# A unit of attention inserted in two places instead of three, its last two steps in the gate's or the value's memory bank

## The chip, the cores and the metric

One NeuronCore of a Trainium2 chip runs the whole program. The time is in device microseconds (us), from three executions of each kernel; their median is what the prediction is about. TensorE (PE) multiplies matrices into PSUM, a memory of eight banks of 128 x 512 numbers; VectorE (DVE) and ScalarE (ACT) read results from there; SyncE (SP) issues the transfers.

## What is computed

Local attention with a few global tokens, followed by two feed-forward layers:

```python
# 4 batches, 8 heads, 512 local and 32 global tokens, 64 per head
out_g = softmax(q_g k_all^T / 8) v_all
out_l = softmax([q_l k_g^T, q_l k_l^T masked to |i - j| <= 32] / 8) [v_g, v_l]
x = rows of out_g, out_l              # 2176 x 512 (heads side by side)
x = (silu(x w_gate) * (x w_val)) w_out        # inner width 1536
out = prelu(x w_in, alpha) w_out2             # inner width 2048
```

All numbers are float32; the weights are split into a high and a low part, and each product of the feed-forward layers is made of three passes (high x high, high x low, low x high).

## The kernel before, in words

The program has three stages. In the first (up to about 405 us of the profiled execution) attention and the first feed-forward layer run interleaved; in the second and third, a blocked product with fewer multiplications finishes the first layer and does the second layer. The change lies in the first stage alone.

`visit1` goes over the twelve blocks `f` of the inner width for one batch of 512 tokens: a gate product (12 matmuls of 128 x 512 into bank `g`), its SiLU on ACT into `sg`, a value product (12 matmuls into bank `v`), the product of both on DVE (`t`), a split of it into high (ACT) and low (DVE) part `h`, and a product with the output weights (`down`, 12 matmuls into the banks `acc0` to `acc3`). Three batches are done in this way, 36 blocks in all. Ahead of each of the three products `pump()` is called. It may insert a step of attention, and it always moves the preparation of the weights on: a load, a conversion of 64-bit numbers on ACT and DVE, a split, a store.

Attention of batches 1 to 3, and the global tokens of all batches, is a list of 20 units: 12 `Local` (a pair of heads) and 8 `Global`. A unit has four parts on PE: `s` (scores into the banks `a0` and `a1`; then a masked maximum on DVE and an exponential on ACT), `t` (eight or six transposes of the exponentials, copied by ACT to `pt`), `pv` (the product with the values; DVE scales it into `o`), and `to` (a transpose of `o`, copied out by ACT). `apump` runs one step of a pipeline over units: step 0 the scores of unit k, step 1 the transposes of unit k-1, step 2 `to` of unit k-3 and `pv` of unit k-2. `pumper` says how many steps are due by each call. Every part takes its bank from `att_bank`, which alternates between `a0` and `a1`. Attention of batch 0 stands ahead of all this (the head) and is spread over all banks.

None of this is issued at once. `Planner` records every instruction of the first stage and then lists them by engine, from the data dependencies, a due time and a cost for each; an instruction that must not be split from its neighbours is in one `atom`. So what the code says is an order of wishes, and the order on an engine is the planner's; it stands below in the part on the change. Nearly every instruction of this stage bears line L273 in the profile, the line at which the planner issues; the tiles' names tell them apart. The names: `g<-xa,w` gate product, `v<-xa,w` value product, `acc<-h,w` down product, `a<-qk` scores, `a<-ident,e` transposes of exponentials, `a<-v,pt` value product of attention, `a<-ident,o` the last transpose.

Of the kernel before, what the change touches and what calls it, by code (L numbers as in the profile page):

```python
# [31 lines left out]
GWIN = (1, 4, 13, 15, 7, 10)  # L32
NG = len(GWIN)
P = dict(
    SLACK=60.0, LOOK=0.1, SWITCH=4.0, MARGIN=0.5, HEAT=8, TINY=90, ND=3, NR=3, LAG=6,
    wr0=0.75, wr2=0.5, wr3=0.75, wr4=0.6, wr5=0.2,
    ns1=33, ns2=34, ns3=32, g1=1.0, g2=1.1, g3=1.0,
    lo0=0.0, lo1=0.0, lo2=0.0, lo3=0.0, hi0=0.0, hi1=0.25, hi2=0.25, hi3=0.5,
    wl0=2, wl1=2, wd=2, tsim=False,
    hq0=0.0, hq1=0.0, hq2=0.0, hq3=0.0, pr_s=0, pr_pv=0, pr_conv=0, pr_hilo=0, pr_st=0, pr_ld=0, pr_h=0,  # L40
# [282 lines left out]
def kernel(  # L323
# [13 lines left out]
    HEAT, ND, NR, LAG = (P[i] for i in ("HEAT", "ND", "NR", "LAG"))  # L337
# [51 lines left out]

    att_tags = {"list": ["a0", "a1", "acc0", "acc1", "acc2", "acc3", "g", "v"], "i": 0}  # L390

    def att_bank():
        t = att_tags["list"][att_tags["i"] % len(att_tags["list"])]
        att_tags["i"] += 1
        return bank(t)
# [49 lines left out]
    class Local(Unit):  # L445
# [59 lines left out]
                nc.vector.reciprocal(out=rc[:, :, 0], in_=rc[:, :, 0])  # L505

        def pv(self):
            o = att_bank()
            with nc.atom():
                for t in range(4):  # L510
                    for h in range(2):
                        for c in range(4):
                            nc.tensor.matmul(
                                out=o[32 * c:32 * c + 32, 128 * t + D * h:128 * t + D * h + D],
                                lhsT=self.pt[:, h, 128 * t + 32 * c:128 * t + 32 * c + 32],
                                rhs=self.pair.v[:, h, 4 * t + c],
                                start=True,
                                stop=True,
                            )
            rc = self.rc  # L520
            self.o = attp.tile([128, 8, D], F32, tag="o", name="o", bufs=1)
            nc.vector.tensor_tensor(
                out=self.o, in0=o.rearrange("p (a d) -> p a d", d=D), in1=rc.to_broadcast([128, 8, D]), op=ALU.mult
            )

        def to(self):
            b, p = self.pair.b, self.pair.p
            t = att_bank()
            rows = self.o.rearrange("p a d -> p (a d)")
            with nc.atom():  # L530
                for i in range(0, 512, 128):
                    nc.tensor.transpose(t[:, i:i + 128], rows[:, i:i + 128], ident)
            if b == 0:
                hi, lo = (xa[:, i, p, 0:S] for i in range(2))
                nc.scalar.activation(out=hi, in_=t, func=ACTF.Copy)
                nc.vector.tensor_tensor(out=lo, in0=t, in1=hi, op=ALU.subtract)
            elif b < B - 1:
                nc.scalar.activation(
                    out=yp[b][:, :, p], in_=t.rearrange("p (a c) -> p a c", a=2), func=ACTF.Copy
                )  # L540
            else:
                for hf in range(2):
                    nc.scalar.activation(out=yh(b, hf)[:, p], in_=t[:, 256 * hf:256 * hf + 256], func=ACTF.Copy)

    class Global(Unit):
# [58 lines left out]
                nc.vector.reciprocal(out=rc, in_=rc)  # L604

        def pv(self):
            o = att_bank()
            with nc.atom():
                for i, w in enumerate(GWIN):
                    for j in range(4):  # L610
                        nc.tensor.matmul(
                            out=o[32 * j:32 * j + 32, 0:D],
                            lhsT=self.pt[:, 128 * i + 32 * j:128 * i + 32 * j + 32],
                            rhs=self.pairs[j // 2].v[:, j % 2, w],
                            start=(i == 0),
                            stop=(i == NG - 1),
                        )
            rc = self.rc
            self.o = attp.tile([128, 8, D], F32, tag="o", name="og", bufs=1)
            for h in range(2):  # L620
                nc.vector.tensor_scalar(
                    out=self.o[:, h], in0=o[:, 0:D], scalar1=rc, scalar2=None, op0=ALU.mult
                )

        def to(self):
            t = att_bank()
            nc.tensor.transpose(t[:, 0:128], self.o.rearrange("p a d -> p (a d)")[:, 0:128], ident)
            ks, cols = slice(2 * self.grp, 2 * self.grp + 2), slice(32 * self.b, 32 * self.b + 32)
            for h in range(2):
                rows = slice(D * h, D * h + D)  # L630
                src = t[rows, 0:128].rearrange("p (k h q) -> p k h q", k=2, h=2)[:, :, h]
                nc.scalar.activation(out=yg[rows, ks, cols], in_=src, func=ACTF.Copy)
# [4 lines left out]
    for b in range(B):  # L637
        for g in range(2):
            if b:
                units += [Local(pairs[b][p]) for p in (2 * g, 2 * g + 1)]  # L640
            units.append(Global(b, g))
        mark.append(3 * len(units))

    st = {"k": 0, "head": True, "w2": 0.0, "w2i": 0}
    due = {}
    rest = {f: deque(pairs[b][p] for b in range(1, B) for p in range(4)) for f in ("load_qk", "load_v")}

# [10 lines left out]
                    getattr(rest[f].popleft(), f)()  # L658

    def apump(mid=None):  # L660
        k, m = divmod(st["k"], 3)
        u, v, w, x = (units[i] if 0 <= i < len(units) else None for i in (k, k - 1, k - 2, k - 3))
        if m == 0 and u:
            u.s()
            later(1, lambda: reload_pairs(u, "load_qk"))
        if m == 1 and v:
            v.t(0)
            v.t(1)
        if m == 2 and x:
            x.to()  # L670
        if m == 2 and w:
            w.pv()
            later(1, lambda: reload_pairs(w, "load_v"))
        for f in due.pop(st["k"], []):
            f()
        if mid:
            mid()
        st["k"] += 1
# [8 lines left out]

    def dbl_tile():
        i = ring["d"] = (ring["d"] + 1) % ND
        if i == 2 and st["k"] < mark[2] - 4:  # L690
            return yp[2].rearrange("p h m c -> p (h m c)").bitcast(I64)
        return dblp.tile([128, 1024], I64, tag="dbl", name="dbl")

# [13 lines left out]
    def wload(now=False):  # L707
        if wq and not wq[0][3]:
            keys, src, pool, _, age = wq[0]
            if st["w"] < age + P["wage"] and not now:  # L710
                return False
            wq.popleft()
            at = pool.next("w")
            t = wtile(pool)
            if callable(src):
                src(t, at)
                return True
            with pr("ld"):
                nc.sync.dma_start(out=t.bitcast(F32), in_=src)
            put(keys, t)  # L720
            return True
        if wq and len(wloaded) < (ND if st["k"] < mark[2] - 4 else 2):
            keys, src, pool, _, _ = wq.popleft()
            raw = dbl_tile()
            with pr("ld"):
                nc.sync.dma_start(out=raw.rearrange("p (i c) -> p i c", i=2), in_=src)
            wloaded.append([keys, raw, pool, st["w"]])
            return True
        return False
# [189 lines left out]
    def visit1(b, fs, last, pump, after_f=None, boundary=None):  # L919
# [13 lines left out]
                after_f(f, "o")  # L933

        for i, f in enumerate(fs):
            pump()
            g = bank("g")
            mm12(g, weight((1, f, "g")), 0, S)
            sg = work.tile([128, 512], F32, tag="sg", name="sg")
            with pr("h"):  # L940
                nc.scalar.activation(out=sg, in_=g, func=ACTF.Silu)
            pump()
            v = bank("v")
            mm12(v, weight((1, f, "v")), 0, S)
            if after_f:
                after_f(f, "gv")
            t = work.tile([128, 512], F32, tag="t", name="t")
            h = hs[f] = hp.tile([128, 2, 512], F32R, tag="h", name="h")
            nc.vector.tensor_tensor(out=t, in0=v, in1=sg, op=ALU.mult)
            nc.scalar.activation(out=h[:, 0], in_=t, func=ACTF.Copy)  # L950
            soon.append(lambda h=h, t=t: nc.vector.tensor_tensor(out=h[:, 1], in0=t, in1=h[:, 0], op=ALU.subtract))
            pump()
            if i:
                down(fs[i - 1])
        if boundary:
# [85 lines left out]
    if True:  # L1041
# [44 lines left out]
        def pumper(nslots, target, wrate=1.0, g=1.0):  # L1086
# [1 line left out]
            c = [0]  # L1088
            st["wr"] = 0.0

            def pump():
                c[0] += 1
                goal = k0 + (target - k0) * (min(c[0], nslots) / nslots) ** g
                mid = wpump
# [44 lines left out]
        p = pumper(P["ns2"], mark[3] + LAG, P["wr2"], P["g2"])  # L1139
        visit1(1, GB, False, p, after_f=summing(reload(GA, GB)))  # L1140
        visit1(1, GA, True, p, after_f=summing(lambda f, ps: None), boundary=lambda: xprep(2))
        p = pumper(P["ns3"], mark[4] + 9, P["wr3"], P["g3"])
        visit1(2, GA, False, p, after_f=reload(GB, GA))

        ops1, w3, place, sums = {}, {}, {}, {}
# [23 lines left out]
        def before_third(f, ps):  # L1169
# [12 lines left out]

            wq.append((None, take, wgv, False, st["w"]))
            if f == GB[4]:
                assert st["k"] >= mark[4] + 9
                tags = iter(("e", "e", "pt", "pt"))
                sums.update(x_sums(2, lambda: attp.tile([128, 1024], F32, tag=next(tags))[:, 0:2 * N3]))

# [14 lines left out]
        visit1(2, GB, True, p, after_f=before_third, boundary=third)  # L1203
        while wq:
            wload(True)
        assert st["k"] >= mark[4] + 9 and not stores
        nc.flush()
        attp_pool.release()
        attc.release()
# [376 lines left out]
```

## Time and profile before

| | before |
|---|---|
| median of three runs | 885.64 us (882.5 to 888.14) |
| profiled execution | 882.67 us, span 880.9 us, mean granted clock 0.993 |
| PE busy | 865.6 us (98%) |
| DVE busy | 690.1 us (78%) |
| ACT busy | 527.1 us (60%) |
| DMA of q1 | 238.19 MB, 71.6% of 16 engines |

The span is the time from the first to the last instruction of one profiled execution; the execution's own time lies 1.8 us above it, and 3.0 us below the median of the runs. PE is busy nearly all the time by the profile's count, in which a matmul that waits behind another is busy too; whether PE is at its peak is read from the distance between the starts of matmuls.

### The profile page before, as it was taken

What the parts mean: (1) busy time and instruction counts of PE and PEld (TensorE: products, weight loads), DVE (VectorE), ACT (ScalarE), POOL (GpSimd) and SP (SyncE); (2) the same over time, 40 slices, a digit from 0 to 9 for tenths busy, and PEclk for the clock granted to TensorE, in tenths of its full rate; (3) what the DMA queues carried; (4) which work ended last, traced back from release to release, by engine and by line L of the source; (5) the groups of instructions that cost most, each with busy time, mean ns of one, the idle gap of its engine ahead of it and who ended that gap; (6) DMA issues with size and microseconds to landing.
All of it is one profiled execution on the core that took longest, in us unless ns stands there. A gap on an engine that the chain in (4) does not pass through costs nothing.

```text
span 880.9 us, 17473 instructions
## 1 busy us (share of the span) xinstructions
PE 865.6 (98%) x6946; PEld 750.5 (85%) x6946; DVE 690.1 (78%) x1441; ACT 527.1 (60%) x1051; POOL 0.7 (0%) x6
## 2 busy tenths in 40 slices
PE   7899999999999999999999999999999999999997
PEld 6677778888788777888999999988999988999996
DVE  4897999989877857597766697777896777967776
ACT  6899999878586877654333346343645434553442
POOL 0000000000000000000000000000000000000000
PEclk8999999999999999999999999999999999999999
DMA  9899899899969799985566576364474645585631
GB/s 350 327 399 405 346 363 379 321 366 384 414 240 353 282 334 337 371 296 183 169 246 227 186 273 239 144 244 186 193 279 178 257 168 214 218 301 214 273 144 61
DMA packets 41666, 239.31 MB, mean 272 GB/s; under 512 B 4848, under 2 KB 5488, under 8 KB 19312
## 3 DMA queue, kind: packets, MB, share of 16 engines
q1 hardware_dynamic: 41584, 238.19, 71.6%
q8 instruction: 55, 0.90, 0.4%
q14 instruction: 27, 0.22, 0.1%
HBM read 183.38 MB, written 54.79 MB: 270 GB/s over the span
## 4 chain that ended last, share of the span: by engine, by line
PE 89%; DMA 5%; ACT 2%; DVE 2%; issue 1%; SPq 0%; ACTq 0%; DVEq 0%
PE ps_acc L1456 21%; PE acc L273 11%; PE g L273 10%; PE ps_g L1245 9%; PE ps_v L1245 9%; PE v L273 9%; PE ps_a L1245 8%; PE a L273 6%; PE ps_acc L1302 3%; PE ps_a L1302 2%; DMA dbl<-in_w_dram 1%; DMA qk<-in_qk_dram 1%; DMA w2so<-dbl 1%; DMA w2sx<-dbl 1%; DMA yp<-in_w_dram 1%
## 5 line engine op out<-in xcount | busy, mean ns | idle before, releaser
L1456 PE MATMUL ps_acc<-w,hring 128*128 128x512 f32 x816 | 194.2, 391 | 0.0
L1456 PEld LDWEIGHTS ps_acc<-w,hring 128*128 128x128 f32 x816 | 152.0, 188 | 30.1 <-ACT hring L1425 0.3
L273 PE MATMUL g<-xa,w 128*128 128x512 f32 x432 | 107.7, 397 | 1.0 <-ACT sg L273 0.4
L273 PE MATMUL v<-xa,w 128*128 128x512 f32 x432 | 107.0, 396 | 0.0
L273 PE MATMUL acc<-h,w 128*128 128x512 f32 x432 | 106.1, 394 | 0.0
L1420 ACT ACTIVATE r<-c 128x384 f32<-128x384 f32 (+1 forms) x96 | 47.9, 498 | 93.2 <-DVE c L1253 93.2
L1461 DVE TENSOR_TENSOR oacc<-ps_acc,oacc 128x512 f32<-128x512 f32 x119 | 81.9, 691 | 21.9 <-PE ps_acc L1456 20.7
L273 PEld LDWEIGHTS g<-xa,w 128*128 128x128 f32 x432 | 79.0, 188 | 20.8 <-ACT sg L273 1.5
L273 PEld LDWEIGHTS acc<-h,w 128*128 128x128 f32 x432 | 79.8, 188 | 18.6 <-issue 1.8
L273 PEld LDWEIGHTS v<-xa,w 128*128 128x128 f32 x432 | 79.3, 188 | 18.4 <-issue 1.4
L1425 ACT ACTIVATE hring<-g 128x384 fp32r<-128x384 f32 (+1 forms) x96 | 48.6, 506 | 55.8 <-DVE g L1422 55.5
L1426 DVE TENSOR_TENSOR hring<-g,hring 128x384 fp32r<-128x384 f32 (+1 forms) x96 | 51.1, 532 | 18.9 <-ACT hring L1425 16.1
L1422 DVE SCALAR_TENSOR_TENSOR g<-g,nal,r 128x384 f32<-128x384 f32 (+1 forms) x96 | 56.8, 591 | 10.6 <-ACT g L1421 10.0
L273 ACT ACTIVATE e<-e,mx 128x128 f32<-128x128 f32 (+1 forms) x136 | 57.2, 423 | 10.6 <-DVE mx L273 10.3
L273 ACT ACT_TABLE_LOAD x46 | 59.0, 1283 | 5.6 <-PE g L273 4.1
L1421 ACT ACTIVATE g<-c 128x384 f32<-128x384 f32 (+1 forms) x96 | 47.9, 499 | 13.7 <-DVE hring L1426 13.7
L1245 PE MATMUL ps_g<-xa,w 128*128 128x320 f32 (+1 forms) x288 | 53.4, 319 | 0.2
L1245 PE MATMUL ps_v<-xa,w 128*128 128x320 f32 (+1 forms) x288 | 53.2, 319 | 0.1
L1245 PE MATMUL ps_a<-w 128*128 128x384 f32 (+1 forms) x288 | 51.4, 326 | 0.0
L1245 PEld LDWEIGHTS ps_g<-xa,w 128*128 128x128 f32 x288 | 47.1, 188 | 1.9 <-ACT p L1261 0.4
L1245 PEld LDWEIGHTS ps_v<-xa,w 128*128 128x128 f32 x288 | 46.9, 188 | 1.6 <-DVE u L1269 0.4
L1245 PEld LDWEIGHTS ps_a<-w 128*128 128x128 f32 x288 | 47.9, 188 | 0.1
(209 smaller groups left out, 1403.1 us busy)
## 6 DMA issues: line engine op xcount, KB each, us to landing
dbl<-in_w_dram SPq DMA_DIRECT2D x28, 1024.0 KB, 7.7
w<-w2so SPq DMA_DIRECT2D x24, 1024.0 KB, 5.3
w<-w2sx SPq DMA_DIRECT2D x24, 1024.0 KB, 4.8
w<-w2ss SPq DMA_DIRECT2D x24, 1024.0 KB, 6.8
v<-in_v_dram SPq DMA_DIRECT2D x15, 1024.0 KB, 10.8
qk<-in_qk_dram SPq DMA_DIRECT2D x14, 688.0 KB, 8.7
w2sx<-dbl SPq DMA_DIRECT2D x8, 1024.0 KB, 5.9
w2so<-dbl SPq DMA_DIRECT2D x8, 1024.0 KB, 9.2
```

The lines of the kernel that those rows point to most:

```text
L273: last[o.eng] = getattr(getattr(self.nc, o.eng), o.op)(*o.args, **o.kw)
L1245: nc.tensor.matmul(out=o[:, 0:n], lhsT=left(name, a, k), rhs=x[name][:, b, k, 0:n], start=(i == 0), stop=(i == 5),)
L1302: mm = nc.tensor.matmul(out=o, lhsT=a, rhs=x, start=(first and e == 0 and not second), stop=((j, f, e) == (NF1 // 2 - 1, 0, 2) and i not i ...
L1420: nc.scalar.activation(out=rr, in_=u, func=ACTF.Relu)
L1421: nc.scalar.activation(out=g, in_=u, func=ACTF.Relu, scale=-1.0)
L1422: nc.vector.scalar_tensor_tensor(out=g, in0=g, scalar=nal[:, i:i + 1], in1=rr, op0=ALU.mult, op1=ALU.add)
L1425: nc.scalar.activation(out=hi, in_=g, func=ACTF.Copy)
L1426: nc.vector.tensor_tensor(out=lo, in0=g, in1=hi, op=ALU.subtract)
L1456: nc.tensor.matmul(out=o, lhsT=a, rhs=x, start=(i == 0), stop=(i == 5))
L1461: nc.vector.tensor_tensor(out=oacc[tb], in0=o, in1=oacc[tb], op=ALU.add)
```

## The change

`apump` has two steps instead of three: in step 0 stand `pv` of unit k-2 and the scores of unit k, in step 1 the transposes of unit k-1 and `to` of unit k-2. `pv` and `to` no longer take `a0` or `a1`: they take the bank that `pump` names, `v` ahead of the gate product, `g` ahead of the value product and ahead of `down`. The counts of steps that other rules use (`mark`, `LAG`, the limits for the third buffer of raw weights and for the last sums) are fitted to two steps per unit, and the steps are spread over 35 and 34 calls instead of 34 and 32 in the second and third batch.

```diff
--- before.py
+++ after.py
@@ -32,9 +32,9 @@
-    SLACK=60.0, LOOK=0.1, SWITCH=4.0, MARGIN=0.5, HEAT=8, TINY=90, ND=3, NR=3, LAG=6,
+    SLACK=60.0, LOOK=0.1, SWITCH=4.0, MARGIN=0.5, HEAT=8, TINY=90, ND=3, NR=3, LAG=2,
     wr0=0.75, wr2=0.5, wr3=0.75, wr4=0.6, wr5=0.2,
-    ns1=33, ns2=34, ns3=32, g1=1.0, g2=1.1, g3=1.0,
+    ns1=33, ns2=35, ns3=34, g1=1.0, g2=1.1, g3=1.0,
...
+    def side_bank():
+
+        return bank(st["side"]) if st["side"] else att_bank()
+
     def att_bank():
...
         def pv(self):
-            o = att_bank()
+            o = side_bank()
...
         def to(self):
             b, p = self.pair.b, self.pair.p
-            t = att_bank()
+            t = side_bank()
...
-        mark.append(3 * len(units))
-
-    st = {"k": 0, "head": True, "w2": 0.0, "w2i": 0}
+        mark.append(2 * len(units))
+
+    st = {"k": 0, "side": None, "head": True, "w2": 0.0, "w2i": 0}
...
     def apump(mid=None):
-        k, m = divmod(st["k"], 3)
-        u, v, w, x = (units[i] if 0 <= i < len(units) else None for i in (k, k - 1, k - 2, k - 3))
+        k, m = divmod(st["k"], 2)
+        u, v, w = (units[i] if 0 <= i < len(units) else None for i in (k, k - 1, k - 2))
+        if m == 0 and w:
+            w.pv()
+            later(1, lambda: reload_pairs(w, "load_v"))
         if m == 0 and u:
             u.s()
             later(1, lambda: reload_pairs(u, "load_qk"))
         if m == 1 and v:
             v.t(0)
             v.t(1)
-        if m == 2 and x:
-            x.to()
-        if m == 2 and w:
-            w.pv()
-            later(1, lambda: reload_pairs(w, "load_v"))
+        if m == 1 and w:
+            w.to()
...
-        if i == 2 and st["k"] < mark[2] - 4:
+        if i == 2 and st["k"] < mark[2] - 3:
...
         for i, f in enumerate(fs):
-            pump()
+            pump("v")
             g = bank("g")
...
-            pump()
+            pump("g")
             v = bank("v")
...
-            pump()
+            pump("g")
             if i:
                 down(fs[i - 1])
...
-            def pump():
+            def pump(side):
+                st["side"] = side
                 c[0] += 1
...
-        p = pumper(P["ns3"], mark[4] + 9, P["wr3"], P["g3"])
+        p = pumper(P["ns3"], mark[4] + 4, P["wr3"], P["g3"])
```

The planner makes another order of it. On PE, from the first gate product of the first stage to its last `down` product, attention stood in 63 places between large products, with 18 joints of two parts in one place; now it stands in 52 places with 30 joints. On ACT the table loads fall from 46 to 42. Each instruction of the work itself is there as before, on each engine, with the bank alone changed.

First place, ACT at the start of the first stage, from the high part of the second weight tile on (`sg` is the SiLU, `e` the exponential of a global unit, `pt` the copy of transposes, `raw`, `dbl`, `y`, `yp` conversions of weights, `w` and `h` high parts). Before:

```order
L273 ACTIVATE e_115,sm_117<-e_115,mx_119 128x768
L273 ACT_TABLE_LOAD
L273 ACTIVATE sg_148<-g_103 128x512
L273 ACTIVATE dbl_111<-dbl_111 128x1024
L273 ACTIVATE h_151<-t_150 128x512
L273 ACTIVATE w_135<-raw_132 128x2x512
L273 ACTIVATE y_139<-yp_95 128x1024
L273 ACTIVATE yp_95<-yp_95 128x1024
L273 ACTIVATE pt_123<-a_113 128x512
L273 ACTIVATE pt_123<-a_114 128x256
L273 ACTIVATE sg_148<-g_103 128x512
```

Now:

```order
L273 ACT_TABLE_LOAD
L273 ACTIVATE sg_148<-g_103 128x512
L273 ACTIVATE dbl_111<-dbl_111 128x1024
L273 ACTIVATE h_151<-t_150 128x512
L273 ACT_TABLE_LOAD
L273 ACTIVATE e_115,sm_117<-e_115,mx_119 128x768
L273 ACTIVATE w_135<-raw_132 128x2x512
L273 ACTIVATE y_139<-yp_95 128x1024
L273 ACTIVATE yp_95<-yp_95 128x1024
L273 ACT_TABLE_LOAD
L273 ACTIVATE sg_148<-g_103 128x512
L273 ACTIVATE pt_123<-a_113 128x512
```

The first SiLU now stands ahead of the exponential of 768 columns, two more table loads stand ahead of the second SiLU, and the two copies to `pt` stand behind it. On PE at this place the scores of a local unit stood between the second value product and the third gate product; now the transposes of the first global unit alone stand there.

Second place, PE in the second batch. Before, a `down` product, transposes, a gate product, then the last transpose of a global unit and the value product of a local one, in `a0` and `a1` (a_113, a_114):

```order
L273 MATMUL acc_121<-h_151,w_143 128x512 x3
L273 MATMUL acc_122<-h_151,w_143 128x512 x3
L273 MATMUL acc_125<-h_151,w_143 128x512 x3
L273 MATMUL acc_126<-h_151,w_143 128x512 x3
L273 MATMUL a_114<-ident,e_115 128x128 x4
L273 MATMUL a_113<-ident,e_115 128x128 x4
L273 MATMUL g_103<-xa,w_135 128x512 x12
L273 MATMUL a_114<-ident,o_130 128x128
L273 MATMUL a_113<-v_110,pt_124 32x64 x32
```

Now:

```order
L273 MATMUL g_103<-xa,w_135 128x512 x12
L273 MATMUL acc_121<-h_152,w_143 128x512 x3
L273 MATMUL acc_122<-h_152,w_143 128x512 x3
L273 MATMUL acc_125<-h_152,w_143 128x512 x3
L273 MATMUL acc_126<-h_152,w_143 128x512 x3
L273 MATMUL g_103<-v_110,pt_124 32x64 x32
L273 MATMUL a_113<-ident,e_115 128x128 x4
L273 MATMUL a_114<-ident,e_115 128x128 x4
L273 MATMUL v_129<-ident,o_130 128x128 x4
L273 MATMUL g_103<-xa,w_136 128x512 x12
L273 MATMUL v_129<-xa,w_136 128x512 x12
```

The value product of attention stands in the gate's bank (g_103), joined to the transposes, and the last transpose stands in the value's bank (v_129); one `down` product lies between the gate product and the former, and one gate product between the latter and the value product that takes its bank again.

## Rows read from the trace of the kernel before

**Rows 1.** Waits of TensorE (PE): total us, how many times, longest us.

```profile
PE g L273 <- ACT sg L273: 0.4, 2, 0.2
```

**Rows 2.** Busy us of each engine in one stretch, granted clock, DMA share, GB/s.

```profile
60.00:80.00 20.00, 20.00 (x220) 15.51 (x220) 16.87 (x43) 19.86 (x43) 0.00 (x0) 1.00 1.00 392
```

**Rows 3.** PE in order of time: start us, length us, what, from 157 us.

```profile
157.45 2.88 PE L273 MATMUL v<-xa,w 128*128 128x512 f32 x12
160.17 2.88 PE L273 MATMUL acc<-h,w 128*128 128x512 f32 x12
162.98 1.54 PE L273 MATMUL a<-qk 64*32 64x256 f32 x32
164.45 3.01 PE L273 MATMUL acc<-h,w 128*128 128x512 f32 x12
167.30 2.88 PE L273 MATMUL g<-xa,w 128*128 128x512 f32 x12
...
173.53 3.00 PE L273 MATMUL g<-xa,w 128*128 128x512 f32 x12
176.37 0.27 PE L273 MATMUL a<-ident,o 128*128 128x128 f32 x1
176.57 1.10 PE L273 MATMUL a<-v,pt 128*32 128x64 f32 x64
```

**Rows 4.** PE in order of time, from 294 us.

```profile
294.81 0.27 PE L273 MATMUL a<-ident,o 128*128 128x128 f32 x1
294.84 3.00 PE L273 MATMUL g<-xa,w 128*128 128x512 f32 x12
```

**Rows 5.** PE in order of time, from 41 to 53 us; idle time before in brackets.

```profile
41.81 3.04 PE L273 MATMUL g<-xa,w 128*128 128x512 f32 x12 [0.20 <-ACT sg L273]
44.69 0.82 PE L273 MATMUL a<-ident,e 128*128 128x128 f32 x6
45.26 2.99 PE L273 MATMUL v<-xa,w 128*128 128x512 f32 x12
48.97 1.16 PE L273 MATMUL a<-qk 64*32 64x128 f32 x64 [0.72 <-ACT pt L273]
50.05 3.02 PE L273 MATMUL g<-xa,w 128*128 128x512 f32 x12
```

**Rows 6.** ScalarE (ACT) in order of time, from 39 to 49 us.

```profile
39.87 1.28 ACT L273 ACT_TABLE_LOAD   x1
41.16 0.60 ACT L273 ACTIVATE sg<-g 128x512 f32<-128x512 f32 x1
...
44.39 1.06 ACT L273 ACTIVATE w<-raw 128x1024 fp32r<-128x1024 f32 x1 [0.84 <-DVE raw L273]
45.97 1.15 ACT L273 ACTIVATE y<-yp 128x1024 f32<-128x1024 f32 x1 [0.52 <-DMA yp<-in_w_dram]
...
48.07 0.85 ACT L273 ACTIVATE pt<-a 128x512 f32<-128x512 f32 x2
48.81 0.60 ACT L273 ACTIVATE sg<-g 128x512 f32<-128x512 f32 x1
```

**Rows 7.** PE in order of time: one gate product, one value product of attention.

```profile
132.83 3.02 PE L273 MATMUL g<-xa,w 128*128 128x512 f32 x12
...
370.73 0.88 PE L273 MATMUL a<-v,pt 128*32 128x64 f32 x48
```

**Rows 8.** ACT in order of time: the SiLU of two gate products.

```profile
142.77 0.60 ACT L273 ACTIVATE sg<-g 128x512 f32<-128x512 f32 x1
...
171.56 0.60 ACT L273 ACTIVATE sg<-g 128x512 f32<-128x512 f32 x1
```

**Rows 9.** VectorE (DVE) in order of time: the scaling of one value product.

```profile
375.34 0.47 DVE L273 TENSOR_SCALAR o<-a,rc 128x64 f32<-128x64 f32 x2
```

**Rows 10.** TensorE's busy us (instructions), granted clock, DMA share, GB/s in two stretches.

```profile
24.00:28.00 4.00, 2.36 (x86) 1.00 1.00 407
28.00:32.00 4.00, 3.06 (x66) 0.57 0.68 217
```

More of the change, by code (lines that the diff above doesn't have):

```diff
@@ L606, in pv @@
         def pv(self):
-            o = att_bank()
+            o = side_bank()
             with nc.atom():
@@ L625, in to @@
         def to(self):
-            t = att_bank()
+            t = side_bank()
             nc.tensor.transpose(t[:, 0:128], self.o.rearrange("p a d -> p (a d)")[:, 0:128], ident)
@@ L721, in wload @@
             return True
-        if wq and len(wloaded) < (ND if st["k"] < mark[2] - 4 else 2):
+        if wq and len(wloaded) < (ND if st["k"] < mark[2] - 3 else 2):
             keys, src, pool, _, _ = wq.popleft()
@@ L1184, in before_third @@
             if f == GB[4]:
-                assert st["k"] >= mark[4] + 9
+                assert st["k"] >= mark[4] + 4
                 tags = iter(("e", "e", "pt", "pt"))
@@ L1205 @@
             wload(True)
-        assert st["k"] >= mark[4] + 9 and not stores
+        assert st["k"] >= mark[4] + 4 and not stores
         nc.flush()
```

## The prediction

> **What bounds the kernel now.** I read the waits of TensorE first. Its idle time is small and lies nearly all in the first 50 us; a SiLU, for one, makes it wait 0.4 us in the whole program [rows 1]. Then the busy times by stretch: from 60 to 80 us TensorE is busy 20.00 of 20 us, at a granted clock of 1.00, while ACT is busy 19.86 us and the DMA engines all the time [rows 2]. Since a waiting matmul can count as busy, I went to the starts in order of time. Two products of twelve matmuls that follow each other start 2.72 us apart (157.45 to 160.17) [rows 3], and nowhere in the stretch from 50 to 400 us that I went through is a distance longer by more than the small joints counted below and some 0.3 us at single places. So TensorE is the bound of the first stage, and it has no slack: this change can win only by fewer joints or by the few waits at the start, and it can lose wherever TensorE must wait for a bank.
>
> **Joints (likely nothing).** Where attention interrupts large products, the steady distance of 2.72 us grows. Ahead of scores it is 2.81 us (160.17 to 162.98), and the product behind them needs 2.85 us (164.45 to 167.30): 0.09 + 0.13 = 0.22 us for such a place. A place with transposes costs 0.12 us (173.53 to 176.37 is 2.84) [rows 3]. The new order has 11 places fewer (52 for 63): 11 x 0.12 to 0.22 = 1.3 to 2.4 us saved. But it has 12 joints of small parts more (30 for 18). One last transpose followed by a value product takes 0.20 us to the next start (176.37 to 176.57) [rows 3]; the same transpose followed by a large product takes 0.03 us (294.81 to 294.84) [rows 4]. So such a joint costs 0.17 us, and 12 of them 2.0 us. The net is between 0.4 us saved and 0.7 us lost; other kinds of joints I have no row for, and bound each by 0 and 0.25 us, which gives 2.4 us saved to 1.7 us lost. I take 0.
>
> **The start of the stage (1.5 us lost).** Before, between the second gate product (41.81) and the third (50.05) stand transposes, a value product and the scores of a local unit, which waited 0.72 us for a copy on ACT and took 1.08 us [rows 5]. In the new order the scores come behind the third gate product, so TensorE has only the value product and the transposes: from 41.81 the gate product takes 2.88 us, the value product about 2.72, the transposes 0.57, and it is ready at about 48.0. It needs the second SiLU, which empties the bank. Before, that ended at 48.81 + 0.60 = 49.41. Now two more table loads of 1.28 us stand ahead of it, and the copies, 0.74 us from start to start (48.07 to 48.81), fall behind it: 49.41 + 2.56 - 0.74 = 51.2 us. The waits of 0.84 and 0.52 us that ACT had on this way may be covered now, which gives 49.9 [rows 6]. So the third gate product starts between 49.9 and 51.2 for 50.05, with the scores (1.08 + 0.22) still to be done: 1.1 to 2.5 us lost. I take 1.5. As the lower bound I keep 0, since ACT may win more than these two waits.
>
> **Banks between uses (0.5 us lost).** `a0` and `a1` now serve scores and transposes alone, which helps them. In exchange the gate's and the value's bank change hands twice as often: I count 39 hand-overs from a large product to attention and 39 back, and at 67 of the 78 no more than one group of twelve matmuls (2.72 us) stands between. What has to happen in that time: a SiLU ended 1.98 us after its product in one case (167.30 + 2.88 to 171.56 + 0.60) and 7.5 us after in the slowest (132.83 + 3.02 to 142.77 + 0.60) [rows 3, 7, 8]; the scaling of a value product ended 4.2 us after it at its slowest (370.73 + 0.88 to 375.34 + 0.47) [rows 7, 9]. These spread from below to far above 2.72 us, but the planner puts a part only where its own reckoning of ACT and DVE has the bank free, as it did with `a0` and `a1` before, and there it erred by almost nothing: a SiLU made TensorE wait 0.4 us in all [rows 1]. That is the nearest row, so I take 0.5 us; no loss is the lower bound, and the upper one is the second rival.
>
> **What costs nothing.** The four table loads that go (4 x 1.28 = 5.1 us of ACT) [rows 6] lie beside large products, which do not wait for ACT; what could come back through them is inside the start's bound. Loads of the scores' and values' tiles move by a few places in SyncE's queue, past stores of weights; after the start no wait of TensorE names a transfer, and the products in between hide them. The second layer's preparation begins three calls of `pump` later, with the same stores issued in the first stage as before; the products of 300 to 400 us cover it, and if they did not, TensorE would wait for a weight late in that stage. The second and third stages have the same instructions in the same order on TensorE.
>
> **On table loads,** the Trainium skill's page "ScalarE: Activation LUTs" (What ACT_TABLE_LOAD costs) counts a drain of some 1.38 us with each load, about 2.66 us in all. The trace does not agree: the load at 39.87 ends at 41.15, and the SiLU behind it starts at 41.16 [rows 6]. By the page the two loads more would cost the start about 2.8 us more, an estimate, and the sum would be 4.8 us; it stays with the row.
>
> **Sum.** 0 + 1.5 + 0.5 = 2.0 us on the profiled execution's own time of 882.67 us gives 884.7. That execution lies 3.0 us below the median of the runs (885.64), so on medians I forecast 885.64 + 2.0 = 887.6 us, no change by the bound of 1% (8.9 us) that I take as what a measurement of this kernel can tell.
>
> **Rivals.**
> - *No loss at all, or a small win (chance with the forecast 0.82 for all within 1%).* If the start loses nothing and joints win their 2.4 us: 883.2 us. For it: ACT was full where the start is slow [rows 2]. Against it: TensorE, not ACT, sets the distance of products.
> - *Slower: late hand-overs (0.11).* One mechanism: the SiLU is queued on ACT behind conversions or table loads, attention's value product stands in the gate's bank one group later, and TensorE stops. Each SiLU as late as the slowest row costs 7.5 - 2.7 = 4.8 us; 19 of the hand-overs to attention are in the gate's bank with at most one group between. It decides from 6.9 us on (8.9 less the 2.0 of the sum), two of the slowest kind or seven of 1 us. With ten of 1 us it gives 897.6 us. For it: ACT is full from 60 to 80 us [rows 2], and a wait of ACT for a transfer, which the planner prices only roughly, now reaches TensorE. Against it: the 0.4 us [rows 1].
> - *Slower: the clock falls (0.02).* In the start, after a stretch with TensorE busy 2.36 of 4 us, the granted clock was 0.57 over the next 4 us, the lower level of 1.2 GHz for most of it [rows 10]: 0.43 x 4 = 1.7 us lost. Six such falls would be 10.2 us, 899.8 us with the sum. Against it, the wait of 0.72 us at 48 us was not followed by one: from 60 us on the clock is 1.00 [rows 2, 5]. The Trainium skill's page "TensorE: Matmul & The Clock Gate" (A second HAM failure mode: psum-queue depth-cycling) tells of a kernel whose short pauses at changes of PSUM banks made the clock swing between its levels; no stretch of this trace shows that after 60 us.
> - *Faster by over 1% (0.05).* It needs 8.9 us. All waits of TensorE at the start (some 3 us), the joints' 2.4 us and what ACT's relief could free there do not reach it; only a cost that the profile doesn't show would.
>
> **Range.** The lower end is no loss with the joints' win, less 2 us for the runs' scatter: 881. The upper end takes in the bounds of start and joints (2.5 + 1.7) and a few late hand-overs (4 us): 894. Chances: faster 0.05, same 0.82, slower 0.13.
>
> **What would show it.** Right: the third gate product near 50 us with a wait on `sg` before it and the scores behind it; ends of the first stage within 3 us of before; 42 table loads; starts 2.72 us apart elsewhere. Wrong: waits of PE on `sg`, `t`, `o` or a copy of `to`, several of 1 us or more, in the stretch from 60 to 400 us (late hand-overs); a granted clock below 1.00 there; or a wait on a weight near 380 us, which would mean that the later preparation was not hidden.

## The result

The changed kernel takes 890.47 us (median of 10 runs, 886.8 to 892.04) for 883.54 us before (10 runs); the ratio is 1.0064, with a 95% interval of 1.0047 to 1.0082. That is no change by the bound of 1%, and inside the range of 881 to 894, but on the slow side of the forecast: about 5.7 us lost by the ratio, which does not go by the medians alone (they lie 6.9 us apart), where the sum had 2.0. The profiled executions take 890.97 and 882.67 us (spans 889.2 and 880.9).

**Where the time went.** I marked the starts of gate products in both traces (36 in the first stage, of twelve matmuls each). The first starts at 32.89 us (before: 33.17), the fourth at 66.24 (64.00), the last at 401.83 (394.08), and the last matmul of the program at 884.29 (875.99). So of these 8.30 us, the head (all ahead of the first product) gives -0.28, the first to the fourth product 2.52, the fourth to the last 5.51, and all behind it 0.55. Nothing of note happens in the second and third stages.

The waits of TensorE after the change (total us, times, longest us), which answer to [rows 1]:

```profile
PE g L273 <- ACT sg L273: 3.5, 2, 3.1
PE v L273 <- DVE o L273: 2.2, 2, 1.2
...
PE acc L273 <- DVE h L273: 1.2, 3, 0.7
...
PE v L273 <- ACT yg L273: 0.5, 1, 0.5
```

The wait on `sg` was 0.4 us and is 3.5; those on `o`, `h` and `yg` are new. The same in the busy times: 60 to 400 us, first before and then after the change (columns as in [rows 2]: the stretch, its length, then the busy us, with the number of instructions, of PE, its weight loads, DVE, ACT and GpSimd; granted clock, DMA share, GB/s).

```profile
60.00:400.00 340.00, 339.76 (x3380) 272.08 (x3380) 279.32 (x603) 272.02 (x495) 0.00 (x0) 1.00 0.91 346
```

```profile
60.00:400.00 340.00, 335.06 (x3365) 268.05 (x3363) 277.13 (x612) 265.54 (x495) 0.00 (x0) 1.00 0.89 343
```

TensorE had 0.24 us of idle time there and has 4.94, at the same clock of 1.00. ACT and DVE did not become busier (265.54 for 272.02 us and 277.13 for 279.32, with the same work spread over a longer stage): no greater load on them makes TensorE wait, they are late at single places.

**The start.** TensorE from 41 us on, for [rows 5]:

```profile
41.30 3.01 PE L273 MATMUL g<-xa,w 128*128 128x512 f32 x12
44.15 2.89 PE L273 MATMUL v<-xa,w 128*128 128x512 f32 x12
46.87 0.81 PE L273 MATMUL a<-ident,e 128*128 128x128 f32 x6
50.77 4.61 PE L273 MATMUL g<-xa,w 128*128 128x512 f32 x12 [3.08 <-ACT sg L273]
55.22 1.09 PE L273 MATMUL acc<-h,w 128*128 128x512 f32 x4
```

and ScalarE, for [rows 6]:

```profile
42.24 1.28 ACT L273 ACT_TABLE_LOAD   x1
43.53 0.94 ACT L273 ACTIVATE e<-e,mx 128x768 f32<-128x768 f32 x1
44.37 0.19 ACT L273 ACTIVATION_READ_ACCUMULATOR e<-e,mx 128x1 f32 x1
44.47 1.05 ACT L273 ACTIVATE w<-raw 128x1024 fp32r<-128x1024 f32 x1
46.64 1.15 ACT L273 ACTIVATE y<-yp 128x1024 f32<-128x1024 f32 x1 [1.12 <-DMA yp<-in_w_dram]
47.69 1.12 ACT L273 ACTIVATE yp<-yp 128x1024 int32<-128x1024 uint32 x1
48.83 1.28 ACT L273 ACT_TABLE_LOAD   x1
50.12 0.60 ACT L273 ACTIVATE sg<-g 128x512 f32<-128x512 f32 x1
```

The third gate product starts at 50.77 as foretold, with the wait on the SiLU before it and the scores behind it (at 58.87). Of ACT's two waits one went (0.84 us on `raw`) and the other grew from 0.52 to 1.12. But look at the length: this product takes 4.45 us to the next start (50.77 to 55.22) instead of 2.72. The granted clock tells why:

```profile
48.00:52.00 4.00, 1.23 (x4) 0.99 (x5) 3.63 (x5) 3.97 (x6) 0.00 (x0) 0.90 1.03 433
52.00:56.00 4.00, 4.00 (x14) 3.17 (x13) 3.97 (x8) 2.63 (x5) 0.00 (x0) 0.68 1.00 345
```

Behind the idle time of 3.1 us it fell to 1.2 GHz for a while: 0.10 x 4 + 0.32 x 4 = 1.7 us, which is the 4.45 - 2.72. All else at the start, the longer wait included (0.72 us before), therefore costs 2.5 - 1.7 = 0.8 us.

**The stretch behind it.** From the fourth to the last gate product I list every distance between two matmuls that is over 0.3 us longer than usual; the excess in us:

| at us | what waits | for | excess |
|---|---|---|---|
| 117 | attention's value product in the gate's bank | `sg` | 0.68 |
| 182, 322, 378 | large product that takes its bank again | `yg`, `y`, `o` | 0.71, 0.36, 1.36 |
| 135 | transposes of the result | `o` (their own input) | 1.18 |
| 165, 201, 242, 244 | `down` | `h` | 0.48, 0.50, 0.45, 0.99 |

That is 6.7 us, for 0.34 us before. The largest shows how such a wait arises (all engines in order of time):

```profile
371.72 1.15 ACT L273 ACTIVATE raw<-dbl 128x1024 f32<-128x1024 f32 x1 [2.78 <-DMA w2ss<-raw]
...
372.34 1.10 PE L273 MATMUL v<-v,pt 128*32 128x64 f32 x64
...
372.90 0.70 DVE L273 TENSOR_SCALAR raw<-raw 128x1024 f32<-128x1024 f32 x1 [2.41 <-ACT raw L273]
...
373.96 1.23 DVE L273 SCALAR_TENSOR_TENSOR dbl<-dbl 128x1024 int32<-128x1024 int32 x1 [0.36 <-ACT dbl L273]
...
375.71 1.21 DVE L273 SCALAR_TENSOR_TENSOR raw<-raw,dbl 128x1024 int32<-128x1024 int32 x1
...
376.84 0.68 DVE L273 TENSOR_TENSOR o<-v,rc 128x512 f32<-128x512 f32 x1
...
377.58 3.02 PE L273 MATMUL v<-xa,w 128*128 128x512 f32 x12 [1.20 <-DVE o L273]
```

Read it from the end. The large product needs the bank `v`, which attention's value product filled by 373.4. DVE could scale it then, but in its order conversions of weights and the low part of `h` stand ahead, and these were late because ACT had waited 2.78 us for a store to free `raw`. Before the change the same store, the seventh to `w2ss` from `raw`, held ACT and DVE up for longer:

```profile
370.69 1.17 ACT L273 ACTIVATE raw<-dbl 128x1024 f32<-128x1024 f32 x1 [4.32 <-DMA w2ss<-raw]
...
371.89 0.69 DVE L273 TENSOR_SCALAR raw<-raw 128x1024 f32<-128x1024 f32 x1 [4.80 <-ACT raw L273]
```

The scaling in [rows 9] stands behind it and ended 4.2 us after its product, and TensorE did not wait. So a late transfer, harmless as long as the value product stood in `a0` or `a1`, now stops TensorE through the bank.

### The profile page after: what moved, and what is told of

Same layout as the page of the kernel before. It is cut to its first block, busy times and chain, and to the rows that moved or that the text cites. A ratio compares the mean times of both kernels' runs of the same rounds, so it can differ in the third digit from the quotient of the medians.

```text
span 889.2 us, 17449 instructions
## 1 busy us (share of the span) xinstructions
PE 865.9 (97%) x6946; PEld 750.1 (84%) x6946; DVE 690.4 (78%) x1441; ACT 523.2 (59%) x1047; POOL 0.7 (0%) x6
## 4 chain that ended last, share of the span: by engine, by line
PE 72%; DVE 12%; DMA 8%; ACT 5%; issue 2%; SPq 0%; DVEq 0%; ACTq 0%
PE ps_acc L1461 21%; PE ps_g L1250 9%; PE ps_v L1250 9%; PE ps_a L1250 8%; PE v L273 6%; PE acc L273 6%; PE g L273 6%; DMA w2ss<-raw 4%; DVE raw L273 3%; PE ps_acc L1307 2%; PE a L273 2%; DVE dbl L273 2%; PE ps_a L1307 2%; DVE y L273 2%; DMA qk<-in_qk_dram 1%
```

## The experiments

All were timed against the kernel before, whose medians beside them were 884.0 to 884.8 us; ratios are to that. "First to fourth" and "fourth to last" are the stretches above (before: 30.83 and 330.08; changed: 33.35 and 335.59), each from the one execution that was profiled. That was the lowest of its row for "only transposes", "three places, value product" and "attention earlier", the highest for "three places, transposes" and the next to highest for "all in the old banks", so a row's stretches need not add up to its median.

| run | median us | ratio, 95% interval | first to fourth | fourth to last |
|---|---|---|---|---|
| changed, again | 890.65 | 1.0072 (1.0048 to 1.0096) | 33.31 | 336.77 |
| all in the old banks | 887.45 | 1.0034 (1.0021 to 1.0048) | 34.55 | 332.33 |
| only value product in new bank | 885.58 | 1.0009 (0.9989 to 1.0029) | 30.46 | 331.16 |
| only transposes in new bank | 891.11 | 1.0070 (1.0043 to 1.0097) | 31.18 | 334.33 |
| three places, value product in new bank | 889.21 | 1.0055 (1.0034 to 1.0076) | 31.37 | 333.73 |
| three places, transposes in new bank | 892.46 | 1.0071 (1.0043 to 1.0098) | 31.59 | 338.66 |
| spare products in the wait | 888.85 | 1.0048 (1.0029 to 1.0067) | 32.45 | 333.57 |
| the same, all in the old banks | 887.75 | 1.0039 (1.0017 to 1.0061) | 31.76 | 333.12 |
| the same, only value product in new bank | 885.04 | 1.0004 (0.9986 to 1.0021) | 31.41 | 330.49 |
| attention earlier | 891.00 | 1.0082 (1.0054 to 1.0109) | 32.13 | 334.10 |
| earlier, only value product in new bank | 888.50 | 1.0052 (1.0031 to 1.0072) | 31.24 | 333.24 |
| margin 1.0 | 890.95 | 1.0072 (1.0046 to 1.0098) | 31.37 | 336.14 |

**Does one trace speak for the others?** The changed kernel a second time.

> The changed kernel once more, for a second trace. Theory 1 (the loss stands at fixed places: the start of the first stage with its clock, and hand-overs of the gate's and value's bank): the wait on the second SiLU near 50.8 us is 2.5 to 3.5 us again with a half clock of about 3.4 us behind it, and of the five other waits over 0.5 us at least four stand at the same instructions; the span is 887 to 891. Rival (the waits are scattered by the execution, a transfer that lands late here or there): the wait near 50 us differs by more than 1 us, and most of the others are elsewhere.

The wait near 50 us is 3.00 us, with a half clock behind it (0.77 and 0.80 of it in the two stretches of 4 us from 48 us on, again 1.7 us). All six excesses of 0.5 us and more in the table above came again at the same instructions, in order of time with 0.62, 1.19, 1.08, 0.50, 0.95 and 1.55 us; two of 0.98 and 0.96 us came in addition, both on `sg`. Theory 1 holds: the places are the program's. The largest has the same chain behind it (ACT waited 2.97 us for the store).

**All attention in the two old banks**, in the new order of two places:

```diff
     def side_bank():
-        return bank(st["side"]) if st["side"] else att_bank()
+        return att_bank()
```

> Two places per unit as in the change, but the value product and the last transpose take a0 and a1 again. Theory 1 (the loss is the start of the stage, 3.4 us of the 8.3 us between the two profiles, and single late hand-overs of the gate's and value's bank, 3.1 us): the start stays as in the change, with a wait of about 3 us on the second SiLU, the waits of TensorE behind the banks g and v go; 74 places instead of 52 give back up to 1.6 us; 887 to 889 us. Rival (the banks are all of the loss): 883 to 885 us. Rival (a0 and a1 become scarce with two steps, which the banks were to cure): 893 us or more.

1.0034: about half of the loss goes with the banks between uses, in the order that the planner then makes (74 places for 52), and the start stays:

```profile
50.39 1.22 PE L273 MATMUL g<-xa,w 128*128 128x512 f32 x2 [3.01 <-ACT sg L273]
```

Behind it the granted clock was 0.70, 0.50 and 0.95 in three stretches of 4 us from 48 us on, which cost 3.4 us in this trace. Theory 1 gave the right size.

**Only the value product in the new bank** (the transposes back in the old ones), and then the reverse:

```diff
         def to(self):
-            t = side_bank()
+            t = att_bank()
```

> Only the result's transposes go back to the two old banks; the value product of attention stays in the gate's or value's bank. Theory 1 (each hand-over costs alike, those after the value product and those after the transposes): half of the 3 us goes, 888 to 889, the waits of a value product on yg and of a gate product on y are gone, the one on o before a value product stays. Rival (the hand-back after the transposes is the whole of it, since ACT with its queue copies them out while DVE scales the value product): 886 to 887.5. Second rival (a0 and a1 get too few places for scores, transposes and results): 890 or more, with waits of scores or transposes on o, y or yg.

885.58 us, no longer told apart from before, and apart from the changed kernel (the intervals do not meet). That is the first rival, and more than it expected. The wait on `o`, which theory 1 let stay, is gone too; of the hand-overs to and from the value product one long wait is left:

```profile
381.93 0.88 PE L273 MATMUL g<-v,pt 128*32 128x64 f32 x48 [0.71 <-ACT sg L273]
```

```diff
         def pv(self):
-            o = side_bank()
+            o = att_bank()
```

> The other half: attention's value product goes back to the two old banks, the result's transposes stay in the gate's or value's bank. Theory 2 (the transposes in the gate's or value's bank are what costs: they need a result of DVE before them and a copy on ACT after them, inside one bank's pause): 889 to 891 as in the changed kernel, with waits of a value product on yg and of transposes on o. Rival (either half relieves, since it only matters how many hand-overs there are): 885 to 887.

1.0070, as the changed kernel. So with two places the times point at the bank of the result's transposes, not that of the value product. The number of places does not tell the two versions apart: either edit undoes most of the joining, 63 places in the former and 65 in the latter. The trace of the latter does not show the waits that I named: the profiled execution took 886.43 us, the lowest of six, and has, behind the start, waits on `o`, `t`, `w` and `sg` of 0.2 to 0.8 us instead. What makes the median slower than that is not in a trace.

The start of the former version also tells something. ScalarE issues the same instructions in the same order as in the changed kernel from 39 to 50 us, but the transfer to `yp` is there in time, and the SiLU starts 1.6 us earlier (0.6 of it because the second gate product does, 40.69 for 41.30):

```profile
45.01 1.15 ACT L273 ACTIVATE y<-yp 128x1024 f32<-128x1024 f32 x1
46.06 1.17 ACT L273 ACTIVATE yp<-yp 128x1024 int32<-128x1024 uint32 x1
47.24 1.28 ACT L273 ACT_TABLE_LOAD   x1
48.54 0.60 ACT L273 ACTIVATE sg<-g 128x512 f32<-128x512 f32 x1
```

TensorE then waited 2.11 us and kept its clock:

```profile
49.19 1.20 PE L273 MATMUL g<-xa,w 128*128 128x512 f32 x4 [2.11 <-ACT sg L273]
```

```profile
46.00:50.00 4.00, 1.89 (x12) 1.40 (x11) 3.64 (x5) 3.97 (x7) 0.00 (x0) 1.00 1.01 421
50.00:54.00 4.00, 4.00 (x19) 3.33 (x18) 3.98 (x7) 3.80 (x5) 0.00 (x0) 1.00 0.97 396
```

**The old order of three places**, with one of the two in the new bank:

```diff
+    def side_bank():
+        return bank(st["side"]) if st["side"] else att_bank()
...
-            o = att_bank()
+            o = side_bank()
```

> Three places as before; only the value product goes to the gate's or value's bank. Theory 1: the start is that of the kernel before (no wait of 3 us, no fall of the clock after it), a few late hand-overs cost 1 to 2 us: 884 to 886 us. Rival (the banks are all of the loss): half of it or more, 887 to 890 us.

1.0055, in the rival's range; theory 1 missed. But the trace does not show that the banks did it: its execution is the lowest of seven, its long waits (1.71 us before transposes, on `pt`) are in `a0` and `a1`, which the planner's new order uses at other times, and no wait behind the gate's or the value's bank is over 0.3 us from 40 us on. With the transposes instead (the same edit on `t` in `to`):

> The kernel before, in three places, with only the result's transposes in the gate's or value's bank. Theory 2: they cost in this order too, 887 to 889, with waits on o before them or on xa, y or yg behind them. Rival (they cost only where they follow their value product by one place, so here there is a whole step between): 883.5 to 885.5, like before.

1.0071, more than theory 2 had, and the transposes wait not on `o` but on the SiLU that must empty the bank first. ACT came to that SiLU late, behind a store and a table load:

```profile
223.37 1.13 ACT L273 ACTIVATE raw<-dbl 128x1024 f32<-128x1024 f32 x1 [3.08 <-DMA w2ss<-raw]
...
225.55 1.28 ACT L273 ACT_TABLE_LOAD   x1
...
226.84 0.60 ACT L273 ACTIVATE sg<-g 128x512 f32<-128x512 f32 x1
...
227.50 0.72 PE L273 MATMUL g<-ident,o 128*128 128x128 f32 x4 [2.73 <-ACT sg L273]
```

```profile
224.00:228.00 4.00, 1.27 (x9) 0.80 (x7) 3.44 (x4) 3.41 (x4) 0.00 (x0) 1.00 1.03 429
228.00:232.00 4.00, 4.00 (x13) 3.15 (x12) 3.90 (x12) 2.36 (x4) 0.00 (x0) 0.58 1.01 426
```

Transposes in the gate's bank stand behind the SiLU of the product before, and large products behind the transposes. Here one hand-over cost 2.7 us of waiting and 0.42 x 4 = 1.7 us of clock. Both versions of this order are slower; that the value product in the new bank costs nothing is seen with two places alone.

**The start by itself.** Twelve spare products of `h` into an accumulator's bank that is not in use yet fill the wait:

```diff
+            if b == 0 and f == 1:
+                warm(12, hs[0][:, 0])
```

> The change with twelve spare matmuls of 128 x 512 put where TensorE waits for the second SiLU (2.7 us of work, whose result nobody reads). Theory 1 says that the wait cost twice: itself (3.1 us) and the half clock after it (1.6 us). With TensorE busy the clock stays at 1.00 behind the wait, and the time falls by 1 to 1.6 us, to about 889 us, while the third gate product starts at the same time. Rival (the clock falls for another reason): no change or up to 0.5 us more, 890 to 891 us.

The clock stays at 1.00, of the wait 1.09 us is left, and 888.85 us is as foretold, though its interval overlaps that of the changed kernel, and the trace has more of the gain behind the start (333.57 for 335.59) than in it (32.45 for 33.35), where the planner's order differs too. With all attention in the old banks too:

> Both suspects taken away at once: all attention in the two old banks again, and twelve spare products in the wait of the third gate product. Theory 1 (start and hand-overs are all of it, and they add): 1.0064 less 0.0030 less about 0.0016 is 1.0018, 885 to 887 against 884.8 before, and no half clock behind 40 us. Rival (the two places themselves cost, because the chain from scores to the last transpose is now shorter by two steps and whatever is taken away comes back as another wait): 888 or more, with new waits of 1 us on pt, o or t.

No half clock, but 887.75, no better than without the spare products; a wait of scores on `o` in the old banks has 1.04 us for 0.62 there. Theory 1 missed: the two costs do not simply add. And with only the value product in the new bank:

> Transposes in the old banks, and twelve spare products in the wait of the third gate product. Theory 1 (the wait of 2.3 us there is a loss of its own that spare work cannot give back, and this order showed no half clock behind it): 885 to 886, within 0.1% of the version without spare products. Rival (the wait is filled and the clock stays up, so 1 us or more comes back): 883 to 884.5. Second rival (another order of the planner brings waits elsewhere): 887 or more.

885.04, as theory 1: here, where the clock had not fallen, spare work gave nothing back.

**Attention earlier,** so that it stands beside the third gate product:

```diff
-    ns1=33, ns2=35, ns3=34, g1=1.0, g2=1.1, g3=1.0,
+    ns1=33, ns2=35, ns3=34, g1=0.85, g2=1.1, g3=1.0,
```

> The change with the attention steps of the first batch due earlier (exponent 0.85 instead of 1), so that scores of a local unit and a value product stand ahead of the third gate product again. Theory 1: the wait of 3.1 us at 47 to 51 us goes or shrinks under 1 us, and with it the half clock behind it; 886 to 888 us, unless the 50 table loads (42 in the change) bring new waits. Rival (the start's wait was covered and only the hand-overs count): no change, 890 us.

The wait of 3 us and the half clock are gone, and a value product waits 1.18 us for `pt` at 50 us instead, another large product 0.71 us for `o` at 70. The median is no better. With 0.9, and the transposes in the old banks:

> Transposes in the old banks, and attention of the first stage begun a little earlier (0.9 for 1.0), so that scores or a value product stand beside the third gate product. Theory 1 (start and hand-overs are all there is to lose, and both are mended): the wait near 47 us falls from 2.3 us below 1 us, 882 to 884, faster than before by up to 0.2%. Rival (as with 0.85 in the changed kernel: parts that come earlier wait on pt and o instead): 886 to 889 with waits of 1 us on pt or o near 50 to 70 us.

The wait is 0.94 us, but behind it come three of 1.3 to 1.6 us between 108 and 120 us, on `yp`, `mx` and `o`: the rival, at another place than it said. The banks are those of the version at 885.58, so the planner's order alone made a difference of 0.4% here.

**A larger margin in the planner:**

```diff
-    SLACK=60.0, LOOK=0.1, SWITCH=4.0, MARGIN=0.5, HEAT=8, TINY=90, ND=3, NR=3, LAG=2,
+    SLACK=60.0, LOOK=0.1, SWITCH=4.0, MARGIN=1.0, HEAT=8, TINY=90, ND=3, NR=3, LAG=2,
```

> The planner must leave 1.0 us instead of 0.5 between the reckoned end of a result on ACT or DVE and TensorE's use of it. Theory 1: the waits between 60 and 410 us, 5 to 6 us in the changed kernel, fall below 2.5 us, the start keeps its 3 us and its half clock; 886 to 888 us. Rival A (what is late is late by more than a margin can buy, transfers and table loads): waits unchanged in sum, 889 to 891. Rival B (the planner moves parts so far that other costs come, a late unit at the stage's end): over 891.

890.95 us and waits as long as without it (0.95 us on `h` at 245, for one; 5.54 us of idle time from 60 to 400 us for 4.94): rival A. The start did not stay as theory 1 had it: the wait is 1.85 us, with no half clock behind it. That half a microsecond does not cover what is late by a transfer is how I read it; no run tells the kinds of lateness apart.

No version beats the kernel before; the best of them are level with it. Taken together: all six orders with the transposes in the new bank (the changed kernel among them) are slower by 0.5 to 0.8%; of the six without, two are level (only the value product in the new bank, with and without spare products) and four are slower by 0.3 to 0.6%. So no order with the transposes in the new bank was level, and an order alone can cost nearly as much.

## Why the prediction was right, and where it was not

- **TensorE bounds the stage and has no slack: right.** The waits of the stretch behind the start (6.7 for 0.34 us) appear in the time, nearly in full.
- **Joints, 0: the sign was open, and a little was won.** 6.4 us more waits, but 5.5 us more time from the fourth to the last product: 0.9 us saved, inside the bounds, if I count all waits rightly. It is a difference and was not measured by itself.
- **Start, 1.5 us: place and mechanism right, the size at its upper bound by luck.** 50.77 lies in the stretch from 49.9 to 51.2. The 2.52 us are 0.8 of waiting, less than the 1.1 to 2.5 of the working, and 1.7 of a clock that fell, which stood only among the rivals. The wait on a transfer to `yp`, which I had hoped would be covered, grew.
- **Banks between uses, 0.5 us: this term failed.** "There it erred by almost nothing" took the 0.4 us on `sg` as the planner's error. But before, attention's own results were late too and nothing waited for `a0` and `a1`; the row measured the planner where it had room. The hand-overs cost 3.1 us in the trace (0.68 + 0.71 + 0.36 + 1.36), and giving the old banks back, in another order of the planner, took away 0.0030 of the 0.0064. Which half of attention pays is not settled by the trace: 2.0 of the 3.1 us are the value product's (0.68 + 1.36), which by the times costs nothing in the order where it alone keeps the new bank.
- **Not in the sum at all:** the transposes one place behind their value product, which wait for its scaling (1.18 us), and `down` products that wait for `h` (2.4 us). I had looked for the price of two places instead of three at the joints alone. The cause of the late `h` was not tried.
- **Costs of nothing:** 42 table loads, and no wait on a weight near 380. The wait at 377.58 is on `o`; a store of the second layer's preparation stands behind it. But these stores (`w2ss`) did not hold ACT up more than before: 9.4 us in four waits, for 9.8 us in four. Nor did the preparation begin later, as the prediction had it: its first store goes out at 161.8 us for 171.2. What changed is that TensorE depends on what stands behind such a store.
- **My own test said so.** The end of the first stage was to lie within 3 us of before; the last gate product starts 7.75 us later. The verdict "within 1%" held because the bound is wide, with two thirds of the loss outside the sum (2.0 of 5.7 us). The time of 887.6 us looks nearer to 890.47 than the change was: its base, 885.64 of three runs, lay 2.1 us above the 883.54 of ten.
- **Rivals.** Late hand-overs was the right mechanism: waits on three of the four tiles that it named (`sg`, `o`, the copies), two of them above 1 us. With 3.1 us, or 4.3 with the transposes' own wait, it stayed below its point of decision of 6.9 us. The clock fell once and cost the 1.7 us that it was priced at, not six times. (Six falls on top of 887.6 give 897.8 us, not 899.8, which counts the sum's 2.0 twice. And the waits before, which the last rival puts at some 3 us, are 1.6 us from the first gate product to 60 us and 8.7 ahead of it, in the head.)
- **Table loads.** The load at 48.83 lasts 1.28 us and the SiLU starts at 50.12: again there is no drain, of which the Trainium skill's page "ScalarE: Activation LUTs" (What ACT_TABLE_LOAD costs) counts some 1.38 us with each load.
- **Changes of banks and the clock.** All short waits of 60 to 400 us, up to 1.20 us of idle time, left the clock at 1.00. So this kernel does not bear out what the Trainium skill's page "TensorE: Matmul & The Clock Gate" (A second HAM failure mode: psum-queue depth-cycling) tells of frequent short pauses; nine in 340 us may be too few to be called frequent.

What stays open: each edit is measured together with the order that the planner makes of it, and nine of these eleven versions came out slower by 0.3 to 0.8%. No run moves a bank and keeps the order, so how much of the loss is the banks' and how much the order's is not shown. That the transposes cost and the value product does not, with two places, is told by times; why, no wait in a trace shows.

## What to carry over

A row with no wait shows that a planner errs little only if something waited for what it planned: before a resource is shared, look at how late its users were while nobody cared. A hand-over of a bank has two sides, the engine that must empty it before and the one that must empty it behind; price both from the queues of these engines, with the transfers that their other work waits for. When two things are moved together, move each alone: here one half, undone, gave back the whole loss. But where a planner makes a new order of every edit, try more than one order before the edit gets the credit: with the same banks, one order was level and another 0.5% slower.

## What the runs showed of the hardware

In four traces a single idle time of TensorE of 2.7 to 3.1 us (three at the start of the stage, one in its middle) was followed by a stretch at 1.2 GHz, which cost 1.7 us (once 3.4) on top of the wait. Behind the idle times of 1.85, 2.11 and 2.25 us at the same start, in three other traces (margin 1.0, only value product, only transposes in the new bank), the clock stayed at 1.00. In three traces a store for which ACT waited (2.78, 2.97 and 3.08 us) made TensorE idle for 1.20, 1.39 and 2.73 us, through the order of ACT and DVE and a bank that one of them had to empty.
